# Float64 weights converted by pairs of matrices on ScalarE and VectorE, and the split of nine groups by subtraction

## The chip, the cores and the metric

The kernel runs on one core of one Trainium2 chip. The metric is the device time of one execution in microseconds (us). Engines are named as in the profile: PE is TensorE, DVE is VectorE, ACT is ScalarE, POOL is GpSimd, SP is SyncE. Each runs its own instructions in order.

## The reference

Three stages, each fed by the one before:

```python
# attention with a decaying complex state: 4 x 8 heads, 768 steps, 48 wide
S_re, S_im = (ar * S_re - ai * S_im + k[t] v[t]^T, ar * S_im + ai * S_re)
y[t] = q[t] @ S_re
# gated layer on x (3072 x 384): w_a, w_b are 384 x 1536, w_out is 1536 x 384
x2 = ((x @ w_a) * (x @ w_b)) @ w_out
# eight experts, top 1: w1 is 8 x 384 x 1024, w2 is 8 x 1024 x 384
e = argmax(x2 @ w_gate);  out = gate * (relu(x2 @ w1[e]) @ w2[e])
```

The weights of the gated layer come as float64, which no engine computes with. The kernel loads them as pairs of 32-bit words and makes float32 values on the chip.

## The kernel before, in words

The 3,072 tokens go in 12 blocks of 256, and a block in two chunks of 128 (below: chunk 0 and chunk 1 of block 0). For a block, `pre` computes the decays and scales q and k with them (products at L1289); the DMA then writes transposed copies qT and kT (`turn`, L1296 to L1300, on SP's queue, and for block 0's qT on ACT's). `attn` makes the scores (sc_p, L1349), masks them, transposes k (kn_p, L1358), multiplies with v (y_p, L1388) and carries the state (kv_p, L1408). Its result x goes through the gated layer by 12 groups f of 128 hidden columns: ab_p is x with w_a and w_b of the group, g their product, and o sums g with w_out of the group. The experts follow at the end.

The 36 matrices of 128 x 384 (a, b and o of each group) pass through two functions:

- `conv` (L877) loads the raw words (384 KB, one DMA on SP) into a room, and DVE makes the float32 matrix in three passes: `shift` (L897), `low` (L900) and `sign` (L903). Rooms are places in which later the low parts of the weights stand; the first six pairs and three double rooms for o are free at once. For an o matrix the gate's weights are folded in beside it (fold): PE transposes it (wt_p, L916), ACT copies it (L920), PE multiplies it with w_gate (wg_p, L926) and ACT puts the result in eight more columns (L929).
- `parted` (L936) splits the matrix into a rounded high part and a rest for products in the faster fp32r form: ACT writes the negative (`less`, L946), a DMA of POOL adds the float32 value to it (`rest`, L949, wL), and ACT writes the high part (`high`, L953).

Block 0 uses the unsplit matrices in plain float32 (`up32`, L979, and `down32`, L985; for the first four groups chunk by chunk). All later blocks use the split ones (L971, L1014), three products for one.

The order of all instructions up to the last expert stage comes from a planner, the class `Plan` (L343): each step is added with a length, the things it reads and writes, and a wanted time `at`; `run` takes, engine by engine, the step that can start and has the smallest `at`. The table `TIMES` shifts (and stretches) `at` for kinds of steps. It holds no times of the chip; it only sets the order. `column` (L1291) copies three columns of the decays within the tile, on DVE. The last function that matters is the end of `expert`: each tile of 128 tokens of an expert's result is scaled by ACT or DVE and scattered by POOL; the very last tile is cut in halves, ACT (L818) and DVE (L819).

## Time and profile before

| | |
|---|---|
| median of 3 runs | 896.99 us (896.51, 896.99, 898.57) |
| the profiled execution | 897.96 us, its span 896.2 us, mean granted clock 0.998 |
| busy: PE, DVE, ACT, POOL | 850.6 (95%), 562.2 (63%), 479.7 (54%), 318.3 (36%) us |
| DMA | 120.28 MB, mean 134 GB/s, first tenth of the span 231 to 273 GB/s |
| chain that ended last | PE 92%, DVE 3%, DMA 3%, SP's queue 1%, ACT 1% |

The page gives the busy time of each engine and its share of the span; the digits of its second part are tenths of busy time in 40 slices of 22.4 us. PE is at 9 in all slices but the first two and the last. The timeline gives start, duration, line, operation and the idle time ahead of it in square brackets. The table of waits adds up that idle time by what ended it. In a DMA row the last number is the time from the issue to the landing of the data.

### The profile page before, as it was taken

To read this page: it belongs to the slowest core of one execution; us is meant where nothing else is said; L and a number is where in the kernel's file an instruction comes from. 1 tells how busy PE (TensorE), PEld (TensorE's weight loads), DVE (VectorE), ACT (ScalarE), POOL (GpSimd) and SP (SyncE) were. 2 spreads that over 40 slices of the span, in tenths; PEclk is the share of its full clock that TensorE was granted. 3 is DMA by queue.
4 is the path that set the end of the run, shared out by engine and by line. 5 is a ranking of instruction groups with operands and counts; after the bars stand their busy time and mean duration, and the time that the engine had idled before them with its cause. 6 is when DMAs were issued, how large, how long until landed. Compare 5 with 4: busy or idle time off the path is not lost.

```text
span 896.2 us, 20677 instructions
## 1 busy us (share of the span) xinstructions
PE 850.6 (95%) x8186; PEld 815.9 (91%) x8186; DVE 562.2 (63%) x1285; ACT 479.7 (54%) x915; POOL 318.3 (36%) x309
## 2 busy tenths in 40 slices
PE   0399999999999999999999999999999999999997
PEld 0387899999999999999999999999999999999996
DVE  6999996775647567484939576345563655455541
ACT  6478787674746456564646473224452544444441
POOL 2341441323363636354353545221123223234111
PEclk9999999999999999999999999999999999999999
DMA  9999975242324272734354453403444454454510
GB/s 253 267 273 259 231 147 151 76 112 66 115 49 131 62 221 46 193 92 124 117 154 132 93 156 81 125 2 111 156 116 128 143 161 136 144 171 125 163 61 24
DMA packets 133017, 120.28 MB, mean 134 GB/s; under 512 B 35964, under 2 KB 127434, under 8 KB 132911
## 3 DMA queue, kind: packets, MB, share of 16 engines
q1 hardware_dynamic: 121519, 100.60, 39.7%
q0 software_dynamic: 9664, 17.47, 8.4%
q8 instruction: 66, 1.08, 0.5%
q10 hardware_dynamic: 1728, 0.79, 0.4%
q14 instruction: 40, 0.33, 0.1%
HBM read 82.48 MB, written 10.61 MB: 104 GB/s over the span
## 4 chain that ended last, share of the span: by engine, by line
PE 92%; DVE 3%; DMA 3%; SPq 1%; ACT 1%; issue 0%; POOL 0%; ACTq 0%; POOLq 0%
PE ab_p L971 31%; PE o L1014 16%; PE o L810 13%; PE h_p L778 12%; PE sc_p L1349 4%; PE y_p L1388 4%; PE ab_p L979 3%; PE o L985 2%; PE kv_p L1408 2%; PE kn_p L1358 1%; PE tn_p L755 1%; DMA q<-in_q_dram 1%; DMA qT<-A 1%; DMA raw<-in_moe_w_dram 1%; DMA raw<-in_moe_w_a_dram 1%; SPq L1138 0%
## 5 line engine op out<-in xcount | busy, mean ns | idle before, releaser
L971 PE MATMUL ab_p<-xH,wL 128*128 128x256 f32 x792 | 221.7, 280 | 0.0
L971 PEld LDWEIGHTS ab_p<-xH,wL 128*128 128x128 f32 x792 | 148.9, 188 | 0.0
L1005 POOL TENSOR_TENSOR gL<-g,gH 128x256 fp32r<-128x256 f32 x96 | 80.0, 835 | 172.3 <-ACT gH L1001 165.6
L994 ACT COPY g<-ab_p 128x256 f32<-128x256 f32 x132 | 48.9, 371 | 136.8 <-PE ab_p L971 124.0
L997 DVE TENSOR_TENSOR g<-g,ab_p 128x256 f32<-128x256 f32 (+1 forms) x148 | 60.5, 409 | 94.0 <-ACT g L994 92.0
L971 PE MATMUL ab_p<-xH,waH 128*128 128x256 f32 x396 | 114.0, 288 | 0.0
L971 PE MATMUL ab_p<-xL,waH 128*128 128x256 f32 x396 | 111.4, 281 | 0.0
L971 PE MATMUL ab_p<-xL,wbH 128*128 128x256 f32 x396 | 110.9, 280 | 0.0
L971 PE MATMUL ab_p<-xH,wbH 128*128 128x256 f32 x396 | 110.8, 280 | 0.0
L1014 PE MATMUL o<-woH,gH 128*128 128x392 f32 x264 | 96.5, 365 | 0.0
L1014 PE MATMUL o<-wL,gH 128*128 128x392 f32 x264 | 90.0, 341 | 0.0
L1014 PE MATMUL o<-woH,gL 128*128 128x392 f32 x264 | 89.9, 341 | 0.0
L810 PE MATMUL o<-w2H,h 128*128 128x384 f32 (+3 forms) x312 | 86.4, 340 | 0.0
L778 PE MATMUL h_p<-sH,w1H 128*128 128x256 f32 (+6 forms) x240 | 77.4, 322 | 0.2 <-DVE hL L789 0.2
L778 PE MATMUL h_p<-sH,w1L 128*128 128x256 f32 (+6 forms) x240 | 76.9, 321 | 0.0
L778 PE MATMUL h_p<-sL,w1H 128*128 128x256 f32 (+6 forms) x240 | 76.8, 320 | 0.0
L971 PEld LDWEIGHTS ab_p<-xH,waH 128*128 128x128 f32 x396 | 74.8, 189 | 0.9 <-issue 0.2
L1001 ACT ACTIVATE gH<-g 128x256 fp32r<-128x256 f32 x132 | 54.5, 413 | 38.5 <-DVE g L997 35.3
L971 PEld LDWEIGHTS ab_p<-xL,waH 128*128 128x128 f32 x396 | 74.7, 189 | 0.4
L971 PEld LDWEIGHTS ab_p<-xH,wbH 128*128 128x128 f32 x396 | 75.0, 189 | 0.0
L971 PEld LDWEIGHTS ab_p<-xL,wbH 128*128 128x128 f32 x396 | 74.8, 189 | 0.0
L824 POOL DMA_INDIRECT out_dram<-ye,ids x29 | 29.9, 1032 | 112.1 <-ACT ye L823 99.9
(211 smaller groups left out, 2135.8 us busy)
## 6 DMA issues: line engine op xcount, KB each, us to landing
raw<-in_moe_w_dram SPq DMA_DIRECT2D x64, 384.0 KB, 3.4
x2d<-x SPq DMA_DIRECT2D x24, 196.0 KB, 3.3
q<-in_q_dram SPq DMA_DIRECT2D x24, 192.0 KB, 4.5
v<-in_v_dram SPq DMA_DIRECT2D x24, 192.0 KB, 4.1
raw<-in_moe_w_a_dram SPq DMA_DIRECT2D x12, 384.0 KB, 6.8
raw<-in_moe_w_b_dram SPq DMA_DIRECT2D x12, 384.0 KB, 5.4
raw<-in_moe_w_out_dram SPq DMA_DIRECT2D x12, 384.0 KB, 7.4
wL<-a POOLq DMA_DIRECT2D x24, 192.0 KB, 6.8
```

Source lines behind the costliest of these rows:

```text
L778: nc.tensor.matmul(out=t, lhsT=lh[:, o:o + 128], rhs=rh[:, kk], start=n == 0, stop=n == 8)
L810: nc.tensor.matmul(out=G["o", c], lhsT=lh, rhs=rh, start=f == 0 and n == 0, stop=f == NH - 1 and n == len(ops) - 1)
L824: d = nc.gpsimd.indirect_dma_start(out, bass.IndirectOffsetOnAxis(ap=ids[0:r, c:c + 1], axis=0), y[0:r], None, bounds_check=NT - 1, oob_is ...
L971: nc.tensor.matmul(out=t[:, i], lhsT=lh[:, kk * 128:(kk + 1) * 128], rhs=rh[:, kk], start=n == 0, stop=n == 8)
L979: nc.tensor.matmul(out=t[:, i], lhsT=A32[nm, f][:, kk * 128:(kk + 1) * 128], rhs=xT["F", 0][:, kk, cs[0]:cs[0] + len(cs)].rearrange("p c t ...
L994: nc.scalar.copy(out=G["g", j, f], in_=G["ab", j, f][:, 0])
L997: nc.vector.tensor_tensor(out=G["g", j, f], in0=G["g", j, f], in1=G["ab", j, f][:, 1], op=ALU.mult)
L1001: nc.scalar.activation(out=G["H", j, f], in_=G["g", j, f], func=ACTF.Copy)
L1005: eng.tensor_tensor(out=G["L", j, f], in0=G["g", j, f], in1=G["H", j, f].bitcast(F32), op=ALU.subtract)
L1014: nc.tensor.matmul(out=G["o", j, c], lhsT=lh[:, c * C:(c + 1) * C], rhs=rh, start=f == first and n == 0, stop=f == last and n == 2)
L1349: nc.tensor.matmul(out=S["p", hg][:, h], lhsT=pq["k", j][:, hg * 4 + h, c, :], rhs=pq["q", j][:, hg * 4 + h, c, 0:C], start=True, stop=True)
L1388: nc.tensor.matmul(out=t[q4 * 32:q4 * 32 + 32, kk], lhsT=a, rhs=b, start=f0, stop=f1)
```

## The change

1. `conv` treats a and b of a group as one matrix "ab" of 768 columns (two raw loads into one room), and o alone. There are six rooms of each kind (FIRST = 3 and three reused). DVE's three passes become an ACT pass and two of DVE: ACT turns the low word into a float in a fixed binade whose last bits are the three that the high word lacks (`tail`), and DVE xors the shifted high word in (`body_`) and then sign and top bits (`head`).
2. `parted`, for the groups f < 9, drops the accumulating DMA: ACT writes the high part, DVE subtracts it (`taken`). Groups 9 to 11 keep the old way, a pair at a time.
3. `column` goes from DVE to ACT. The last output tile is scaled whole by ACT.
4. The table `TIMES` has other numbers and other entries, so that most of the order of the first 120 us is new.

```diff
+DIRECT = 9
-FIRST = (6, 3)
+FIRST = 3
+BY_TAIL = {"ab": 0, "o": 0}
+TAIL = (7.49 * 2.0 ** -55, -2.0 + 2.0 ** -23)
...
-    ('pre', 0, 1, 0): (-32.6, 1),
-    ('pre', 0, 1, 1): (18.2, 2.16),
+    ('pre', 0, 1, 0): (-175.1, 1),
+    ('pre', 0, 0, 2): (-165.1, 1),
...
-                            elif e == NE - 1 and c == nt - 1:
-                                nc.scalar.activation(out=y[0:r, 0:DM // 2], in_=G["o", c][:, 0:DM // 2], func=ACTF.Copy, scale=gt[0:r, c])
-                                nc.vector.tensor_scalar(out=y[0:r, DM // 2:DM], in0=G["o", c][:, DM // 2:DM], scalar1=gt[0:r, c], scalar2=None, op0=ALU.mult)
...
+        SIZE = dict(ab=2 * 384, o=384 + NE)
+        def room(f):
+            return f if f < FIRST else FIRST + (f - FIRST) % (NF // 2 - FIRST)
...
+            def tail():
+                held()
+                nc.scalar.activation(out=K["a"].bitcast(F32), in_=K["lo"], func=ACTF.Copy, scale=TAIL[0], bias=TAIL[1])
+            def body_():
+                nc.vector.scalar_tensor_tensor(out=K["a"], in0=K["hi"], scalar=3, in1=K["a"], op0=ALU.logical_shift_left, op1=ALU.bitwise_xor)
+            def head():
+                nc.vector.scalar_tensor_tensor(out=K["a"], in0=K["hi"], scalar=0x7FFFFFFF, in1=K["a"], op0=ALU.bitwise_or, op1=ALU.bitwise_xor)
...
+            if nm in BY_TAIL and f >= BY_TAIL[nm]:
+                P.add("ACT", on("ACT", m), tail, kind="tail", r=mine, w=[slot], at=at)
+                P.add("DVE", on("DVE", m), body_, kind="conv", r=mine, w=[slot], at=at)
+                P.add("DVE", on("DVE", m), head, kind="conv", r=mine, w=[slot, done], at=at)
...
+            def taken():
+                nc.vector.tensor_tensor(out=W["L", nm, f], in0=A32[nm, f], in1=W[nm, f][0], op=ALU.subtract)
+            if f < DIRECT:
+                P.add("ACT", on("ACT", n), high, kind="less", r=[slot, ("A32", nm, f)], w=[mine, ("W", nm, f)], at=at)
+                P.add("DVE", on("DVE", n), taken, kind="taken", r=[slot, ("A32", nm, f), ("W", nm, f)], w=[own, ("L", nm, f)], at=at + SPLIT[2])
+                return
...
-                        nc.vector.tensor_copy(out=(ld[x, j] if x == "q" else PT[x, j])[:, :, lo:hi, C:C + 1], in_=T("A")[:, :, :, C - 1:C])
+                        nc.scalar.copy(out=(ld[x, j] if x == "q" else PT[x, j])[:, :, lo:hi, C:C + 1], in_=T("A")[:, :, :, C - 1:C])
```

The order changes most in the first 50 us. On SP, before, from the last two raw loads of the first twelve (L890 and L888 are raw loads; the first six kT are the transposed copies of chunk 0, the next six those of chunk 1):

```order
L890 DMA raw<-in_moe_w_b_dram 128x3x256
L888 DMA raw<-in_moe_w_out_dram 128x768
L1300 DMA kT<-Bt 16x8x128 x3
L1300 DMA kT<-k 16x8x128 x3
L890 DMA raw<-in_moe_w_a_dram 128x3x256
L890 DMA raw<-in_moe_w_b_dram 128x3x256
L888 DMA raw<-in_moe_w_out_dram 128x768
L890 DMA raw<-in_moe_w_a_dram 128x3x256
L1300 DMA kT<-Bt 16x8x128 x3
L1300 DMA kT<-k 16x8x128 x3
L890 DMA raw<-in_moe_w_b_dram 128x3x256
L888 DMA raw<-in_moe_w_out_dram 128x768
```

In the change (raw loads are L908 and L906) the same place, up to chunk 0's kT (im is an input of the attention):

```order
L908 DMA raw<-in_moe_w_b_dram 128x3x256
L906 DMA raw<-in_moe_w_out_dram 128x768
L1195 DMA im<-in_a_im_dram 128x3x256
L908 DMA raw<-in_moe_w_a_dram 128x3x256
L908 DMA raw<-in_moe_w_b_dram 128x3x256
L906 DMA raw<-in_moe_w_out_dram 128x768
L908 DMA raw<-in_moe_w_a_dram 128x3x256
L908 DMA raw<-in_moe_w_b_dram 128x3x256
L906 DMA raw<-in_moe_w_out_dram 128x768
L1355 DMA kT<-Bt 16x8x128 x3
L1355 DMA kT<-k 16x8x128 x3
```

Four raw loads of groups 4 and 5 that stood behind chunk 0's kT, and two that stood behind chunk 1's, now stand ahead of both, so that eighteen raw loads and not twelve come first.

On PE, before, from the second fold to kn_p (a_383 is o1, wt_p and wg_p are the fold):

```order
L916 MATMUL wt_p<-ident,a_383 128x128 [waits DVE_49]
L916 MATMUL wt_p<-ident,a_383 128x128 x2
L926 MATMUL wg_p<-wg,wt 32x8 [waits Activation_49]
L926 MATMUL wg_p<-wg,wt 32x8 x11
L1349 MATMUL sc_p<-qT,kT 128x128 [waits DMAHW4_49,DMAHW3_49,DMAHW5_49,DMAHW2_49,DMAHW6_49,DMAHW1_49,DMAHW7_49,DMAHW0_49,PE_49]
L1349 MATMUL sc_p<-qT,kT 128x128 x3
L1349 MATMUL sc_p<-qT,kT 128x128 [waits PE_49]
L1349 MATMUL sc_p<-qT,kT 128x128 x3
L1358 MATMUL kn_p<-ident,kT 128x96 [waits Activation_49]
L1358 MATMUL kn_p<-ident,kT 128x96 x3
L1358 MATMUL kn_p<-ident,kT 128x96 [waits DVE_49]
L1358 MATMUL kn_p<-ident,kT 128x96 x3
```

In the change, from the third fold (a_330 is o2, a_342 is o3):

```order
L955 MATMUL wt_p<-ident,a_330 128x128 [waits DVE_49,PE_49]
L955 MATMUL wt_p<-ident,a_330 128x128 x2
L965 MATMUL wg_p<-wg,wt 32x8 [waits Activation_49]
L965 MATMUL wg_p<-wg,wt 32x8 x11
L1404 MATMUL sc_p<-qT,kT 128x128 [waits DMAHW4_49,DMAHW3_49,DMAHW5_49,DMAHW2_49,DMAHW6_49,DMAHW1_49,DMAHW7_49,DMAHW0_49,PE_49]
L1404 MATMUL sc_p<-qT,kT 128x128 x3
L955 MATMUL wt_p<-ident,a_342 128x128 [waits DVE_49,PE_49]
L955 MATMUL wt_p<-ident,a_342 128x128 x2
L1404 MATMUL sc_p<-qT,kT 128x128 [waits DVE_49]
L1404 MATMUL sc_p<-qT,kT 128x128 x3
L1413 MATMUL kn_p<-ident,kT 128x96 [waits Activation_49]
L1413 MATMUL kn_p<-ident,kT 128x96 x3
```

One more fold stands ahead of the first scores, and the transposes of a fourth stand between their two halves.

On DVE, in the change, around the scans of block 0 (L1289, whose results scale q and k; L930 and L933 are the two xors, L1001 the subtraction; a_233 and a_288 are pairs, a_307 is o1):

```order
L1279 SCALAR_TENSOR_TENSOR Bt<-X,Bt 128x3x128 [waits DVE_49]
L930 SCALAR_TENSOR_TENSOR a_288<-raw,a_288 128x768 [waits DMAHW7_49,DMAHW0_49,Activation_49]
L1001 TENSOR_TENSOR wL<-a_233,wabH_256 128x768
L1289 SCALAR_TENSOR_TENSOR X<-zeros,X 128x128 [waits Activation_49]
L1289 SCALAR_TENSOR_TENSOR X<-zeros,X 128x128 x2
L933 SCALAR_TENSOR_TENSOR a_288<-raw,a_288 128x768 [waits DVE_49]
L1328 SCALAR_TENSOR_TENSOR X<-X 128x3x128 [waits Activation_49]
L930 SCALAR_TENSOR_TENSOR a_307<-raw,a_307 128x384 [waits DMAHW1_49]
L1329 TENSOR_SCALAR carry<-X 128x3 [waits DVE_49]
L933 SCALAR_TENSOR_TENSOR a_307<-raw,a_307 128x384 [waits DVE_49]
L1289 SCALAR_TENSOR_TENSOR X<-zeros,carry,X 128x128 [waits DVE_49]
L1289 SCALAR_TENSOR_TENSOR X<-zeros,carry,X 128x128 x2
```

The xors of a pair and the first subtraction now stand ahead of the first scans; before, the 128x384 pass L897 of b0 and a reduction stood just ahead of them.

## Rows read from the trace of the kernel before

**Rows 1.** The page, part 1: busy us, share of the span, instructions.

```profile
PE 850.6 (95%) x8186; PEld 815.9 (91%) x8186; DVE 562.2 (63%) x1285; ACT 479.7 (54%) x915; POOL 318.3 (36%) x309
```

**Rows 2.** Waits of PE: waited for, us in total, times, longest.

```profile
PE wt_p L916 <- DVE a L903: 33.9, 2, 26.3
PE ab_p L979 <- ACT x L1393: 1.1, 1, 1.1
PE sc_p L1349 <- issue: 0.5, 1, 0.5
PE ab_p L979 <- DVE g L997: 0.5, 1, 0.5
```

**Rows 3.** Timeline of PE: start, us, line, operation, count [idle before].

```profile
37.35 0.90 PE L916 MATMUL wt_p<-ident,a 128*128 128x128 f32 x3 [7.65 <-DVE a L903]
38.82 0.51 PE L926 MATMUL wg_p<-wg,wt 128*32 128x8 f32 x24 [0.57 <-ACT wt L920]
39.36 3.76 PE L1349 MATMUL sc_p<-qT,kT 96*128 96x128 f32 x16
...
47.52 1.60 PE L979 MATMUL ab_p<-x,a 128*128 128x128 f32 x12 [1.08 <-ACT x L1393]
...
52.64 1.95 PE L1349 MATMUL sc_p<-qT,kT 96*128 96x128 f32 x16
```

**Rows 4.** DMA: SP's issue, landings of windows 20.9:22 and 32.8:33.3, the page's wL.

```profile
20.92 1.03 SPq L888 DMA_DIRECT2D raw<-in_moe_w_out_dram  x1
...
raw<-in_moe_w_out_dram SPq DMA_DIRECT2D x1, 384.0 KB, 9.9
...
kT<-k SPq DMA_DIRECT2D x1, 64.0 KB, 2.0
...
wL<-a POOLq DMA_DIRECT2D x24, 192.0 KB, 6.8
```

**Rows 5.** Windows: busy us of PE, PEld, DVE, ACT, POOL; clock, DMA share, GB/s.

```profile
25.00:30.00 5.00, 1.38 (x27) 0.92 (x27) 4.11 (x9) 1.77 (x5) 3.34 (x3) 1.00 1.08 350
30.00:35.00 5.00, 0.00 (x0) 0.00 (x0) 5.00 (x13) 3.06 (x5) 1.28 (x1) 1.00 0.69 155
60.00:80.00 20.00, 19.50 (x172) 14.81 (x171) 19.72 (x46) 16.71 (x38) 5.89 (x6) 1.00 1.04 280
```

**Rows 6.** Timeline of DVE, conversion of two matrices.

```profile
32.59 0.62 DVE L897 TENSOR_SCALAR a<-raw 128x384 uint32<-128x384 uint32 x2
33.13 1.02 DVE L900 SCALAR_TENSOR_TENSOR a<-raw,a 128x384 uint32<-128x384 uint32 x2
34.06 1.35 DVE L1289 TENSOR_TENSOR A<-q,X 128x384 f32<-128x384 f32 x1
```

**Rows 7.** Groups, busy and mean ns: DVE subtraction and ACT roundings.

```profile
L678 DVE TENSOR_TENSOR w1L<-raw,w1H 128x768 fp32r<-128x768 f32 x32 | 30.7, 958 | 6.8 <-ACT w1H L677 6.1
...
L677 ACT ACTIVATE w1H<-raw 128x768 fp32r<-128x768 f32 x32 | 26.9, 840 | 2.1 <-DMA raw<-in_moe_w_dram 2.1
...
L946 ACT ACTIVATE wL<-a 128x384 fp32r<-128x384 f32 (+1 forms) x36 | 18.2, 526 | 1.1 <-DVE k L1289 0.8 <-DVE a L903 0.3
```

**Rows 8.** Timeline of PE, places of one wg_p and one wt_p.

```profile
67.70 0.38 PE L926 MATMUL wg_p<-wg,wt 128*32 128x8 f32 x24
68.00 1.58 PE L985 MATMUL o<-a,g 128*128 128x392 f32 x4
69.43 0.49 PE L916 MATMUL wt_p<-ident,a 128*128 128x128 f32 x3
69.75 1.50 PE L979 MATMUL ab_p<-x,a 128*128 128x128 f32 x12
```

**Rows 9.** Timeline of all engines behind the last matmuls.

```profile
889.62 0.42 ACT L818 ACTIVATE ye<-o,gt 120x192 f32<-120x192 f32 x1 [7.79 <-PE o L810]
890.08 0.42 DVE L819 TENSOR_SCALAR ye<-o,gt 120x192 f32<-120x192 f32 x1 [4.01 <-ACT ye L818]
890.81 1.05 POOL L824 DMA_INDIRECT out_dram<-ye,ids  x1 [3.48 <-DVE ye L819]
```

More of the change, by code (lines that the diff above doesn't have):

```diff
@@ L874, in fast, with behind @@
-        late = [("ab", f) for f in range(FIRST[0], NF)] + [("o", f) for f in range(FIRST[1], NF // 2)]
-        rooms += [late[i % len(late)] for i in range(3 * NF - len(rooms))]
-        def conv(i, f, src, nm, at):
+        SIZE = dict(ab=2 * 384, o=384 + NE)
+        def behind(nm, k, dt, n):
+            return wts.tile([128, 2 * SIZE[nm]], dt, tag=f"l{nm}{k}", name=n)
+        for nm in SIZE:
+            for f in range(NF):
+                wts.tile([128, SIZE[nm]], F32R, tag=f"h{nm}{f}", name=f"w{nm}H{f}")
+            for h in range(NF // 2):
+                behind(nm, h, F32R, "wL")
@@ L885, in load @@
[L885 to L892 removed]
+            slot, mine = ("s",) + (to or (nm, NF)), [("sl", nm, 2 * room(f)), ("sl", nm, 2 * room(f) + 1)]
@@ L1304, in mul @@
                     for x in "Aq":
-                        add("DVE", column(x), ks("A", x), [("column", x, lo)], weight=0.16)
+                        add("ACT", column(x), ks("A", x), [("column", x, lo)], weight=0.2)
                 add(e, times, ks(src, "Cc" if c2 == 0 else "F"), ks(t))
```

223 lines of the change are left out of this document (124 added, 99 removed).

## The prediction

> **What bounds the kernel now.** I read the page's busy times first: TensorE is busy for 850.6 of 896.2 us [rows 1]. Only PE's clock of work matters, then, and nothing is won on another engine unless PE waits for it. The waits of PE come next [rows 2]: 33.9 us for the last pass of a weight's conversion (L903, all of it before 39.4 us), and after that 1.1, 0.5 and 0.5 us in three single places. The whole rest of the 800 us runs without a wait worth a row. So a change that keeps PE's instructions can move the time in three places only: the instant at which PE starts for good, the few waits after it, and the end behind the last matmul. Both programs give PE the same matmuls, 6,546 by the two orders and of the same shapes (8,186 records in the profile, where an fp32 one counts twice), in another order. Hence the sum below has just these three places, with no term for work.
>
> The instant is read in PE's timeline [rows 3]: the fold of o1 (three transposes wt_p at 37.35, twelve wg_p at 38.82), then the scores of the first chunk, sc_p, from 39.36, and no gap over 0.1 us until a 1.08 us wait at 47.52. The 7.65 us of idle time ahead of wt_p name DVE: the start is set by o1's conversion. The scores' other inputs are the transposed copies kT and qT, made by DMA. The last kT of the first chunk was issued from 32.8 on and landed 2.0 us after its issue [rows 4]: at about 35. They were ready over 4 us before PE used them. Twelve raw weights of 384 KB stood ahead of them on SP; the last of these was issued at 20.92 and landed 9.9 us later, at 30.8 [rows 4]. The DMA engines were full before that (share 1.08, 350 GB/s, from 25 to 30), and not in the next 5 us (0.69) [rows 5]. From 60 to 80 DVE is busy 19.72 us of 20 and ACT 16.71 [rows 5].
>
> **The change part by part.** *Loads.* The rooms of the raws are now six pairs and six single ones, and SP issues eighteen raws, a to o of groups 0 to 5, ahead of the first kT. Six more raws of 393,216 bytes take 1.12 us each at the 350 GB/s of 25 to 30, 1.40 at the 280 of 60 to 80 [rows 5]: 6.7 to 8.4 us. One accumulating DMA of 192 KB that fell into that stretch is gone [rows 4]; it reads its target too, so I count it between half a raw and a whole one, about 1 us. The last raw then lands at 30.8 + 6.7 - 1.0 = 36.5, at most 38.2. Behind it come the chunk's twelve transposes of 64 KB: 0.19 to 0.25 us each by the same rates, 2.3 to 3.0 us. The scores' inputs are complete at 38.8 to 41.2. The slack of 4 us is used up and the two paths to the start are now about equal.
>
> *Conversion ahead of the start.* PE folds three output groups, o0 to o2, before the scores, not two. Up to the last xor of o2, DVE makes three pairs and three single matrices and takes one subtraction (wL from a, L1001). Before it made six matrices there. Per matrix that was L897 at 0.27 us (two from 32.59 to 33.13) and two passes at 0.465 (two from 33.13 to 34.06) [rows 6], 1.2 us, so 7.2 in all. A pass over 768 columns has its nearest row in L678, 0.958 us [rows 7]; less the 0.085 by which consecutive ones overlap (0.55 against 0.465) that is 0.87. Now: six passes of 768, six of 384 and one subtraction, 6 x 0.87 + 6 x 0.465 + 0.87 = 8.9 us. DVE had little idle time there (5.00 us busy of 5 from 30 to 35, 4.11 before [rows 5]), so o2's fold ends 1.7 us later than o1's did: PE starts at 41.1. Four short copies (`column`) leave DVE in that stretch; I set what they give against the new waits of the xors for ACT, which must make the low bits first. The start therefore lies between 39.4 (copies count, raws land at the fast rate) and 42.5 (slow rate, and the last transposes wait for a place on their queue). I take 41.1, where the DVE path ends and which lies within the DMA path's ends: **+1.7 us**, from 0 to +3.1.
>
> *The third fold* is done while PE would be idle: later PE has one wt_p (0.32 us from 69.43 to the next row) and one wg_p (0.30 from 67.70) less [rows 8]: **-0.6**.
>
> *Half speed.* The sixteen passes of the first sc_p took 3.76 us, those of the second chunk 1.95 [rows 3]. The first stretch after the start thus runs at the lower of the clock's two levels. The new order has the same kind of unbroken work there, so it pays the same; a wait among the first scores might lengthen it, which is in the upper end.
>
> *Known waits.* At 47.52 PE waited 1.08 us for the copied x; the new order puts the first kv_p and a wt_p between y_p and this ab_p, and some 0.8 us of the wait is filled. The 0.5 of ab_p behind the product g [rows 2] loses its place. Together **-1.3**. The 0.5 of issue I leave.
>
> *New waits.* The order has five new places where PE takes a result just made: the second half of sc_p, behind o3's wt_p; a wg_p between the kn_p; ab_p of groups 2 and 3 behind their xors; the first product with the split weights, which now needs a subtraction behind ACT's rounding. The nearest rows are the recorded waits of this sort, 0.5 to 1.1 us [rows 2]; at five places 0 to 4 us. I take **+2.0**, 0.4 each, near the smaller of these rows, because PE runs behind its inputs for most of that time.
>
> *Later conversion.* Over all groups DVE loses 36 x 1.2 = 43.2 us, gets 24 x 0.87 + 24 x 0.465 = 32.0 and the nine groups' subtractions, 9 x 0.87 + 9 x 0.48 = 12.2: +1.0, which the 24 short copies outweigh. Hidden behind PE as long as DVE is no later than now; where that cover goes, see the second rival. ACT loses 72 roundings of 0.526 us [rows 7], 0.44 if they overlap as DVE's do (31.7), and gets tails and roundings in 768 columns at 0.84 - 0.085 = 0.755 [rows 7] and in 384 at 0.44: 14.3 for the twelve pairs of tails, 14.3 for the rounding, 3.6 for the three groups that keep the old way, and the copies at about 0.1 each, in sum +2.9 us. With 16.71 of 20 busy [rows 5] ACT has room for it: 0. The Trainium skill speaks against this move: its page "ScalarE: Activation LUTs", section "Rules for kernel authors", gives multiply and add to VectorE and not to ScalarE, because VectorE is faster per element. The rows bear out the speed, 0.84 us for 768 columns against 0.62 for two L897 of 384 [rows 6, 7]; but what counts is who has room. If ACT were the one that PE waits for, the sum would be 2.9 us higher. The thirty accumulating DMAs that go free POOL and the DMA queues, neither of which PE waits for: 0.
>
> *Tail.* The last output tile was scaled in two halves, one after the other: ACT at 889.62, DVE only at 890.08, the scatter issued at 890.81 [rows 9]. Each half took 0.42. Whole, it takes ACT about 0.55 (192 columns take 0.42, 768 take 0.84 [rows 7, 9]); with the 0.31 from the last half's end to the scatter that is 0.86 in place of 1.19: **-0.3**.
>
> **Sum:** 1.7 - 0.6 - 1.3 + 2.0 - 0.3 = +1.5 us. The profiled execution took 897.96 (its span 896.2 and 1.8 around it) and would take 899.5. It is 0.97 above the median of the runs shown, so against that: 896.99 + 1.5 = **898.5 us**. A measurement of this kernel tells about 0.2%, 1.8 us, from no change. The forecast is no change that can be told, with a lean to slower; its own range is 897 to 900.5.
>
> **Rivals.** *The start does not move* (faster). In rows 5 the DMA engines have room from 30 to 35, and the raws are issued earlier now because nothing blocks SP; if the copies' time on DVE counts in full and the xors don't wait for ACT, the start stays at 39.4 to 39.7. With inputs that early all three recorded waits go (1.1 + 0.5 + 0.5) and hardly any comes: 0.3 - 0.6 - 2.1 + 0.3 - 0.3 = -2.4, or -3.0 without the first and the fourth term: 894.0 to 894.6. Against it: the kT stand behind the raws on the same queue, and the subtraction stands ahead of the scans that make k.
>
> *DVE or ACT becomes the engine that PE waits for up to some 115 us* (slower). Every weight now crosses ACT, DVE, ACT and DVE, in order, where it crossed DVE and then ACT beside POOL's DMA. DVE has 0.28 us of room in 20 [rows 5], about 1 us in the 70 up to the last subtraction. Once its idle time for ACT's tails exceeds that, PE gets the excess: 0.2 to 0.4 us in each of twelve groups is 2.4 to 4.8 us, less the 1 us of room, so 900 to 902.3, and with the start at its late end 903. For it: DVE's full row. Against: ACT's tails need only the raw, which is early. An ACT pass over uint32 words with a gap between them is shown by no row; at twice the time it would add 14 us to ACT and give the same picture at its upper end.
>
> *The new waits don't come* (the change's first order is as quiet as the old one): 1.7 - 0.6 - 1.3 - 0.3 = -0.5, with some tenths of waits 896.5 to 897.
>
> **How the numbers follow.** The forecast has 0.50 (0.30 of it within 0.2% of 896.99, that is below 898.8, 0.20 above). The start that doesn't move has 0.19, of which 0.17 is below 895.2 (it may end between). DVE or ACT as the bound has 0.21, all slower. No new waits has 0.10, of which 0.02 is below. So faster 0.19, same 0.40, slower 0.41. The range reaches from the middle of the first rival to the upper part of the second, 894.3 to 902.6, and leaves out about 0.1 on each side.
>
> **What would show it.** In PE's timeline: sc_p's first row at 40.5 to 42 (39.4 to 39.9 for the first rival); twelve transposes landing after the eighteenth raw; three folds ahead of sc_p. In PE's waits after it: several rows of 0.2 to 0.9, together near 2.5 us; over 5, with DVE or ACT named between 60 and 115, the second rival holds. At the end: one ACT row of about 0.55 and the scatter 0.3 us sooner after the last matmul. I would be wrong in kind if PE's busy time or its spacing in the long middle differed.

## The result: 7.4 us slower, and the profile after

The changed kernel takes 904.44 us (median of 5 runs, 902.87 to 907.5), the kernel before, beside it, 896.99 (5 runs, 896.51 to 898.75). The ratio is 1.0075 with a 95% interval of 1.0058 to 1.0092: slower, by more than the forecast's whole range (894.3 to 902.6) allowed. The profiled execution is the longest of the five, 907.5 us with a span of 905.4. It is 9.5 us above the profiled execution before.

The page's part 1, to be laid beside [rows 1]:

```profile
PE 852.5 (94%) x8186; PEld 815.0 (90%) x8186; DVE 563.5 (62%) x1216; ACT 486.9 (54%) x923; POOL 292.7 (32%) x279
```

PE has the same 8,186 records and 1.9 us more busy time; the others moved the way that the edit asks for (POOL 25.6 us less, ACT 7.2 and DVE 1.3 more). So the time is in PE's waits and in the pace of its work, not in its amount. The table of waits of PE (waited for, us in total, times, longest) beside [rows 2]:

```profile
PE wt_p L955 <- DVE a L933: 33.4, 3, 22.3
PE wg_p L965 <- ACT wt L959: 3.7, 3, 1.6
PE o L1069 <- POOL gL L1060: 2.4, 3, 2.0
PE ab_p L1023 <- DVE g L1052: 2.2, 1, 2.2
PE h_p L804 <- DVE hL L815: 2.0, 1, 2.0
PE sc_p L1404 <- issue: 0.8, 1, 0.8
PE rk_p L663 <- DVE oh L640: 0.6, 1, 0.6
PE ab_p L1023 <- DVE xL L1457: 0.4, 1, 0.4
```

The first two rows lie ahead of the first scores. Behind them stood 2.1 us of waits before; now there are 6.4 in the rows of o, ab_p, sc_p, rk_p, and 2.0 more for h_p in the expert stage. None of the three large ones (2.0 of the 2.4 for gL, 2.2, 2.0) was in the forecast. PE's timeline at the head (start, us, line, operation, count, idle time before) beside [rows 3]:

```profile
38.39 0.88 PE L955 MATMUL wt_p<-ident,a 128*128 128x128 f32 x3 [7.00 <-DVE a L933]
40.82 0.51 PE L965 MATMUL wg_p<-wg,wt 128*32 128x8 f32 x24 [1.56 <-ACT wt L959]
41.53 2.05 PE L1404 MATMUL sc_p<-qT,kT 96*128 96x128 f32 x8 [0.20 <-DMA qT<-A]
43.37 0.85 PE L955 MATMUL wt_p<-ident,a 128*128 128x128 f32 x3
44.37 2.08 PE L1404 MATMUL sc_p<-qT,kT 96*128 96x128 f32 x8
...
47.32 0.51 PE L965 MATMUL wg_p<-wg,wt 128*32 128x8 f32 x24 [0.24 <-DVE sm L1408]
...
50.30 1.50 PE L1463 MATMUL kv_p<-v,kn 128*32 128x48 f32 x48
```

The start moved from 39.36 to 41.53, 2.2 us. Beside [rows 3] it falls into three parts: the last fold's wt_p came at 38.39 in place of 37.35 (1.0 us), its wg_p waited 1.56 us for ACT's copy in place of 0.57 (1.0), and sc_p waited 0.20 for qT. The copy stood on ACT behind the issues of qT:

```profile
40.29 0.48 ACT L959 COPY wt<-wt_p 128x384 f32<-128x384 f32 x1 [4.50 <-DMA qT<-q]
```

The second thing to see is the pace. The 48 passes of kv_p take 1.50 us here at 50.30; in the kernel before the same 48 took 0.88:

```profile
49.05 0.88 PE L1408 MATMUL kv_p<-v,kn 128*32 128x48 f32 x48
```

In the change PE still runs at the lower of its two levels (1.2 and not 2.4 GHz): the trace's first record of the full granted clock is at 52.5, 11.0 us after the first scores, where before it was at 45.5, 6.1 us after them. In that stretch lie o3's wt_p between the two halves of sc_p and a wait of 0.24 us. (The windows read 1.00 ahead of that record too; there the passes' own times have to be read.)

The lower level comes back once. Windows of before and then after: start, end, length, busy us of PE, PEld, DVE, ACT, POOL, granted clock, DMA share, GB/s:

```profile
135.00:140.00 5.00, 5.00 (x40) 5.00 (x39) 2.61 (x5) 4.72 (x11) 0.00 (x0) 1.00 0.66 178
```

```profile
135.00:140.00 5.00, 2.77 (x15) 2.57 (x14) 1.56 (x3) 3.84 (x6) 1.72 (x1) 0.79 0.85 267
140.00:145.00 5.00, 5.00 (x40) 4.91 (x38) 4.04 (x7) 3.84 (x6) 0.00 (x0) 0.87 0.47 133
```

Behind the 2.23 us wait of ab_p at 137.77 the passes come 0.21 us apart until 141.26. What held ab_p stands in ACT's timeline:

```profile
136.16 0.84 ACT L1264 ACTIVATE A<-re 128x768 f32<-128x768 f32 x1 [3.24 <-DMA qT<-q]
136.91 0.35 ACT L1049 COPY g<-ab_p 128x256 f32<-128x256 f32 x1
```

The first decay step of block 3 (A<-re) stands ahead of the gate's copy and waits 3.24 us for a transposed copy of block 2. The gate's copy, which PE needs, has nothing to wait for there but its place. The same picture on POOL at 481, for the wait at 483.25:

```profile
472.62 0.98 POOL L686 DMA_INDIRECT idtab<-tok,posu  x1 [0.94 <-DVE acc L675]
...
481.14 0.98 POOL L686 DMA_INDIRECT idtab<-tok,posu  x1 [4.37 <-DMA idtab<-tok,posu]
482.15 1.05 POOL L1060 TENSOR_TENSOR gL<-g,gH 128x256 fp32r<-128x256 f32 x1
```

The second index scatter waits 4.37 us until the first, issued at 472.62, has landed; the low part gL, which the next product needs, stands behind it.

Where the 9.5 us went by time: the first product of the expert stage (h_p), behind which the order is the old one, starts at 653.66, before at 646.14. So 7.5 us are lost up to there, and 2.0 in one wait behind a late expert weight. That last one is not all the change's: the same kernel again had 0.70 there, the kernel before 0.2. For the 7.5, two windows from the first score to h_p, before and then after (columns as above):

```profile
39.36:646.14 606.78, 604.52 (x6653) 578.07 (x6653) 406.27 (x901) 352.91 (x662) 239.62 (x218) 1.00 0.50 130
```

```profile
41.53:653.66 612.13, 605.03 (x6626) 576.04 (x6626) 404.70 (x843) 355.93 (x659) 214.27 (x192) 1.00 0.43 118
```

PE is idle for 7.1 us of its window in place of 2.3, and busy for 605.0 in place of 604.5. So the start gives 2.2, the waits 4.8 and the work 0.5, in sum 7.5. The 0.5 hides larger parts, which I work out from the starts of the passes in the two traces, waits left out. The passes at the lower level took 6.8 us longer than as many of the same kinds at the full level, before 3.2: 3.6 more. The third fold, done ahead of the scores, saves 0.7 behind them. At the full level ab_p and o together took 478.2 us in place of 481.7, 3.5 less, and the other products 1.1 more. Why ab_p and o ran closer together is shown by no run.

The tail did what was forecast: ACT's whole tile takes 0.58 us, and the scatter is issued 0.31 behind its end.

```profile
899.00 0.58 ACT L846 ACTIVATE ye<-o,gt 120x384 f32<-120x384 f32 x1 [7.79 <-PE o L836]
899.89 1.05 POOL L847 DMA_INDIRECT out_dram<-ye,ids  x1 [3.19 <-ACT ye L846]
```

From the start of the last matmul to the end it is 6.73 us, before 7.00.

### The profile page after: what moved, and what is told of

The parts are those of the page before. It is cut to its first block, busy times and chain, and to the rows that moved or that the text cites. A ratio compares the mean times of both kernels' runs of the same rounds, so it can differ in the third digit from the quotient of the medians.

```text
span 905.4 us, 20607 instructions
## 1 busy us (share of the span) xinstructions
PE 852.5 (94%) x8186; PEld 815.0 (90%) x8186; DVE 563.5 (62%) x1216; ACT 486.9 (54%) x923; POOL 292.7 (32%) x279
## 4 chain that ended last, share of the span: by engine, by line
PE 77%; issue 8%; DMA 4%; DVE 4%; POOL 3%; SPq 2%; ACT 1%; POOLq 0%; ACTq 0%; DVEq 0%
PE ab_p L1023 28%; PE o L1069 14%; PE o L836 9%; PE h_p L804 8%; PE sc_p L1404 5%; PE y_p L1443 4%; PE ab_p L1031 3%; DMA raw<-in_moe_w_b_dram 2%; PE kv_p L1463 2%; PE kn_p L1413 1%; PE o L1037 1%; PE tn_p L781 1%; POOL out_dram L847 1%; DMA qT<-A 1%; POOL gL L1060 1%
## 5 line engine op out<-in xcount | busy, mean ns | idle before, releaser
L1023 PE MATMUL ab_p<-xH,wabH 128*128 128x256 f32 x792 | 226.3, 286 | 2.2 <-DVE g L1052 2.2
L1023 PE MATMUL ab_p<-xL,wabH 128*128 128x256 f32 x792 | 221.8, 280 | 0.4 <-DVE xL L1457 0.4
L1023 PEld LDWEIGHTS ab_p<-xH,wabH 128*128 128x128 f32 x792 | 150.2, 190 | 5.2 <-DVE g L1052 3.1
L1023 PEld LDWEIGHTS ab_p<-xL,wabH 128*128 128x128 f32 x792 | 149.8, 189 | 0.8 <-DVE xL L1457 0.6
L1052 DVE TENSOR_TENSOR g<-g,ab_p 128x256 f32<-128x256 f32 x132 | 54.9, 417 | 120.2 <-ACT g L1049 119.8
L1069 PE MATMUL o<-woH,gH 128*128 128x392 f32 x264 | 93.4, 354 | 0.0
L813 ACT ACTIVATE h<-h_p 128x384 fp32r<-128x384 f32 (+4 forms) x48 | 24.5, 510 | 76.4 <-PE h_p L804 76.4
L815 DVE SCALAR_TENSOR_TENSOR h<-h_p,h 128x384 fp32r<-128x384 f32 (+1 forms) x48 | 26.7, 556 | 62.4 <-ACT h L813 62.3
L836 PE MATMUL o<-w2L,h 128*128 128x384 f32 (+3 forms) x168 | 56.8, 338 | 0.0
L836 PEld LDWEIGHTS o<-w2H,h 128*128 128x128 f32 (+3 forms) x312 | 56.3, 186 | 0.5
```

The lines of the kernel that those rows point to most:

```text
L836: nc.tensor.matmul(out=G["o", c], lhsT=lh, rhs=rh, start=f == 0 and n == 0, stop=f == NH - 1 and n == len(ops) - 1)
L1023: nc.tensor.matmul(out=t[:, i], lhsT=lh[:, kk * 128:(kk + 1) * 128], rhs=rh[:, kk], start=n == 0, stop=n == 8)
L1052: nc.vector.tensor_tensor(out=G["g", j, f], in0=G["g", j, f], in1=G["ab", j, f][:, 1], op=ALU.mult)
L1069: nc.tensor.matmul(out=G["o", j, c], lhsT=lh[:, c * C:(c + 1) * C], rhs=rh, start=f == first and n == 0, stop=f == last and n == 2)
```

## The experiments

The runs were made in six groups, each on one chip with the kernel before beside it; all ratios are to that. In most of them a few lines behind the planner take one step out of the finished order and put it behind another step; nothing else is changed. MOVE holds pairs of step numbers (which, behind which):

```python
for a, b in MOVE:
    i = [n for _, n, _ in out].index(a)
    x = out.pop(i)
    out.insert([n for _, n, _ in out].index(b) + 1, x)
```

### Do the waits belong to the order?

**after_again**: no edit.

> The changed kernel once more, for its spread and a second profile. The theory: of the 10.5 us of waits and half-speed work behind the start, the wait at 137.8 us (2.2 us, with 1.7 us of slower passes behind it) belongs to the order and comes again, within 0.5 us; the waits at 245, 431, 483 and 678 us (0.6, 0.8, 2.0, 2.0) hang on single slow transfers and move or vanish. Then the sum of waits behind the start is 5 to 11 us, other than in the first profile in the second half of the span. The rival, that all of them belong to the order: the same waits in the same places. Time 903 to 907.5 by both.

Measured 905.58 us, 1.0074 [1.0054, 1.0094]. The waits came back at the same places and sizes: 0.23 at 47.4, 2.31 at 138.7, 0.58 at 246.2, 1.10 at 432.4, 2.08 at 484.5. Only the 2.0 for an expert weight shrank, to 0.70. So the late waits are the order's own, and my expectation that they are single late transfers was wrong for all but that one.

**late_new3**: the kernel before, whose table gets the change's entries for blocks 3 and later, and nothing else.

```diff
-    ('v', 3): (-41, 1),
-    ('attn', 3, 'PE'): (33.2, 0.77),
...
+    ('pre', 3, 0, 0): (183.3, 1),
+    ('attn', 3, 'PE'): (-83.3, 4.0826),
...
```

> The kernel before, with the new planned times for blocks 3 and later alone; conversion, loads and the first 160 us as before. If the new order of the later blocks is what lets slow transfers reach PE, waits of PE appear behind 160 us, 1 to 4 us in sum, and the time is 898 to 901. If the later blocks' order costs nothing and all of the loss comes from conversion and the first 160 us, the time is that of the kernel before within 1 us (896.5 to 898).

Measured 901.73 us, 1.0037 [1.0018, 1.0055]: 3.3 us lost with the old conversion and the old head. New or longer waits of PE stand at 144.9 (0.85, before 0.55 at 144.6), 186.2 (0.63) and 428.25:

```profile
428.25 1.02 PE L1356 MATMUL sc_p<-qT,kT 96*128 96x128 f32 x7 [1.84 <-DMA qT<-q]
```

So the new entries of the later blocks cost time without the new conversion. But this is a mixed table, new entries behind old ones (best_old4 below is another, and loses more), and its waits are other ones than in the change: how much of the change's loss these entries make is not shown by it.

### The wait at 138

**swap_sqre**: ACT's A<-re of block 3 goes behind the gate's copy, MOVE = ((682, 595),).

> One instruction of ACT moved: the square of block 3's decay (A<-re), which waits for a transfer, now stands behind the next gate copy of block 1 and not ahead of it. The theory, that this one wait holds PE at 137.8 us: the wait shrinks from 2.2 to under 0.5 us, the clock stays at its higher level there, and the time falls by 2.5 to 4 us against the changed kernel of this job. The rival, that DVE's and ACT's load in the conversion stretch sets PE's pace there: the wait comes back at the next gate copy, and the time falls by under 1 us.

Measured 904.57 us, 1.0076 [1.0054, 1.0097]: nothing gained. The wait went on to the next result in line:

```profile
141.22 0.90 PE L1423 MATMUL kn_p<-ident,kT 96*128 96x96 f32 x4 [1.96 <-DVE sm L1418]
```

The cause is one step further. DVE's subtraction of a group waits for ACT's rounding, which is still behind A<-re, and the masks stand behind it and behind two scalings of block 3:

```profile
137.74 0.96 DVE L1011 TENSOR_TENSOR wL<-a,wabH 128x768 fp32r<-128x768 f32 x1 [3.76 <-ACT wabH L1005]
...
140.48 0.68 DVE L1418 TENSOR_TENSOR sm<-sc_p,causal 128x512 f32<-128x512 f32 x1
```

**pre3_late** moves the whole group: ACT's A<-re and the two steps with it behind the rounding, DVE's scalings of block 3 behind both masks.

```diff
+MOVE = (
+    (685, 491),
+    (684, 491),
+    (682, 491),
+    (845, 651),
+    (693, 651),
+    (689, 651),
+    (844, 651),
+    (688, 651),
+)
```

> The changed kernel with block 3's first decay steps behind what block 1 and 2 need: on ACT A<-re stands behind the gate copy and the next rounding, on DVE the two passes of block 3's X stand behind both masks of block 2. The theory, that the order puts an instruction that waits for a late transfer ahead of PE's inputs on both engines: the wait at 138 to 141 us (2.0 to 2.3 in three profiles) falls below 1 us, the clock stays high there, and the time falls by 2 to 4 us. The rival, that DVE and ACT are short of time there (they lost some 9 us of DVE in idle time from 40 to 62): a wait of the same size comes a few us later and the time falls by under 1 us.

Measured 902.82 us, 1.0030 [1.0013, 1.0046]. The wait at 138 is gone (0.15 and 0.45 us are left at 143.7 and 155.3) and with it the fall of the clock.

### The half speed at the head, and the scatter

**fold3_back**: o3's fold goes out of the middle of the first scores, behind y_p: MOVE = ((198, 391), (197, 391), (196, 128), (195, 128)).

> The changed kernel with o3's fold (wt_p, its copy, wg_p) moved from between the first scores to behind the first y_p; nothing else is moved. The theory: the 0.24 us wait of that wg_p at 47.3 us broke PE's unbroken work and kept TensorE at the lower of its two levels until 52.5 to 53.6, where it reached the higher one 6.2 us after the start in the kernel before. Without the wait the full clock comes at 47 to 48.5 and the passes up to 53 take about 2 us less; new waits at kv_p may take up to 1.2 of that. The time falls by 1 to 2.5 us. The rival, that the longer half-speed stretch follows from the later start alone: the clock still comes at 52 or later, and the time stays within 0.5.

Measured 903.38 us, 1.0031 [1.0015, 1.0046]. PE's timeline:

```profile
41.48 3.75 PE L1417 MATMUL sc_p<-qT,kT 96*128 96x128 f32 x16 [0.17 <-DMA qT<-A]
45.02 0.97 PE L1426 MATMUL kn_p<-ident,kT 96*128 96x96 f32 x8
```

The sixteen passes of sc_p run without a break, and kn_p behind them takes 0.97 us for eight. The kernel before took 1.49:

```profile
42.90 1.49 PE L1358 MATMUL kn_p<-ident,kT 96*128 96x96 f32 x8
```

The full level comes at 45.3, 3.8 us after the first scores. This is one execution, and the instant varies: in the three profiles of combo below, which has the same move, it comes 8.7, 6.1 and 3.9 us after them; in the seven profiles of the change's conversion that leave the fold in its place (the change three times, swap_sqre, pre3_late, idtab_late, raws_behind) 8.9 to 12.0. So the fold's place shortens the stretch on the whole, by no fixed amount. Part of the gain goes into a new wait of kv_p for ACT's copy kn at 48.91 (0.96).

**idtab_late**: the second index scatter of each pair goes behind the next three instructions of POOL.

```diff
+        for a in [o["n"] for o in ops if o["kind"] == ("scatter", 1)]:
+            i = [n for _, n, _ in out].index(a)
+            j = [q for q in range(i + 1, len(out)) if ops[out[q][1]]["e"] == "POOL"][2]
+            out.insert(j, out.pop(i))
```

> The changed kernel with the second of each block's two scatters of ids (POOL) moved behind the next three POOL instructions. The theory: the second scatter waits for the first one's landing, 8 us at 474 us, and PE's low part gL stands behind it on POOL; moved, the wait of 1.5 to 2.1 us at 482 to 484 us goes, and the small ones at 334 and 402 us with it, and the time falls by 1.5 to 2.5 us. The rival, that POOL is only late there with everything else: another wait takes its place and the time stays within 0.7 us.

Measured 904.06 us, 1.0035 [1.0019, 1.0052]. The waits for gL at 334 and 483 are gone, 0.25 at 401 stays, and the wait for g at 137 (1.83 us, with the lower level until 140.7) is not.

These three were on one chip without the changed kernel beside them, so what each gave is not to be read from their ratios. That is done with all three together.

### The three moves together

**after_third**: no edit, the yardstick.

> The changed kernel as it is, as the yardstick for the three runs beside it on the same chip. Theory (the order's own waits): 6 to 8.5 us over the kernel before, with the same waits in the same places (0.24 us of wg_p at 47 us, 2.2 near 138, 0.6 near 246, 1 near 432, 2 near 484). Rival (the waits are chance on two chips): places or sizes differ by over half.

Measured 905.80 us, 1.0059 [1.0035, 1.0084]; waits at the same places, 1.91 us at 136.8 this time without a fall of the clock behind it.

**combo**: MOVE holds the pairs of fold3_back and pre3_late, and the scatters move as in idtab_late.

> Three moves together: the third output group's late fold goes behind y_p, the decay step and the scalings of block 3 go behind the gate work, each second index scatter goes three steps of POOL later. Theory (the loss sits in single waits and in the half speed that follows them, and they add): 5 to 7 us below the changed kernel on the same chip, so 1 to 3 above the kernel before, of which 2 are the later start; no half speed after 46 us. Rival (a wait removed comes back at the next result that PE takes): within 2 us of the changed kernel, with new waits of 3 us or more in sum.

Measured 901.97 us, 1.0008 [0.9987, 1.0029], 3.8 us below after_third and 1.2 above the kernel before beside it. Repeated on that chip it took 900.65, 1.0015 [0.9998, 1.0032] (combo_again), and 900.05, 1.0011 [0.9995, 1.0026] (combo_third).

> The three moves together once more, as the yardstick for the two runs beside it. From the first such run: 0 to 2.5 us over the kernel before on the same chip, full clock from 51 us on, no drop after it.

> The three moves alone a third time, as the yardstick for the run beside it: 0 to 2.5 us over the kernel before, the first sc_p at 41.5 us.

Combo's table of waits, the first two rows behind those of the folds:

```profile
PE tn_p L807 <- issue: 1.0, 1, 1.0
PE sc_p L1430 <- issue: 0.9, 1, 0.9
```

The longest wait is 1.02 us there and 1.12 in combo_again. Moving 24 steps (the twelve pairs of MOVE and twelve scatters) takes back 3.8 of the 5.0 us by which the change was slower on that chip. Most of the loss thus sat in places of the order. In this pair of profiles it was the waits: the full level came at 50.5 in combo and at 50.7 in after_third, and PE's idle time from the first score to h_p fell from 7.2 to 4.0 us. How the 3.8 us divide among the three moves is not shown.

**best_old4**: the moves of fold3_back and pre3_late, and for blocks 4 and later the table entries of the kernel before.

> The first two moves (third fold, block 3), and the table's entries for blocks 4 and later are those of the kernel before. Theory (the later blocks' new entries cost 3 us by themselves): no wait of o for gL near 334 and 484, those of 246 and 432 gone or halved, and the time 0.5 to 2.5 us below the three moves alone. Rival (a mixed table is a third order with waits of its own): new waits of 1 us or more behind 200 us in other places, the time 0 to 3 us above the three moves alone.

Measured 908.06 us, 1.0093 [1.0068, 1.0118], beside combo_again 7.4 us slower. The rival held: a mixed table is a third order, with waits of its own between 239 and 275 us (1.82 for gL, 1.84 and 2.00 for g) and the lower level from 250.0 to 256.9. It also leaves the scatters where they were, which combo moves, so the 7.4 us are not the table's alone.

### The two parts of the edit, each undone in the same order

**conv_dve**: DVE converts alone, in the three old passes, at the places of the two xors.

```diff
             def tail():
-                held()
-                nc.scalar.activation(out=K["a"].bitcast(F32), in_=K["lo"], ...)
+                pass
             def body_():
-                nc.vector.scalar_tensor_tensor(out=K["a"], in0=K["hi"], scalar=3, ...)
+                shift()
+                low()
             def head():
-                nc.vector.scalar_tensor_tensor(out=K["a"], in0=K["hi"], scalar=0x7FFFFFFF, ...)
+                sign()
```

> Same order, but the float64 words are converted by DVE alone in its three old passes at the place of the two xors; ACT's pass is left out. Theory (the two-engine conversion does what it is made for, DVE is the fuller engine): DVE gets some 9 us more up to 90 us (12 x 0.5 and 12 x 0.27), PE's first sc_p comes at 43 to 44.5 us, new waits of PE name DVE between 48 and 90, and the time is 3 to 8 us above the changed kernel. Rival (the wait of DVE for ACT's pass costs what the pass saves): sc_p within 0.7 us of 41.5 and the time within 1.5 us of the changed kernel, or below it.

Measured 913.66 us, 1.0139 [1.0105, 1.0173], 7.9 us above after_third, as the theory had it. The first scores came at 42.78, a little sooner than expected, and the waits stand for the most part later than it had them:

```profile
PE ab_p L1031 <- DVE g L1045: 2.0, 3, 1.4
PE ab_p L1023 <- DVE g L1052: 1.8, 1, 1.8
...
PE ab_p L1023 <- DVE xL L1457: 1.3, 1, 1.3
```

They name DVE, in six places between 73 and 145 us. So in this order ScalarE's pass does what it is for. The rule of the Trainium skill that the forecast weighed (page "ScalarE: Activation LUTs", section "Rules for kernel authors": add and multiply belong on VectorE, with a figure for bf16 and one source), taken by itself, speaks for this run, and it was the slower one. But the order was made for the new passes: the old passes in their own order, the kernel before, took 900.77 us on that chip, less than either. What the two conversions are worth in an order made for each is not shown.

**sub_dma**: the first nine groups get their low parts in the old way (ACT writes the negative, here directly behind the high part, and a DMA of POOL adds the value).

```diff
             def high():
...
-                    place()
+                    less()
...
             def taken():
-                nc.vector.tensor_tensor(out=W["L", nm, f], in0=A32[nm, f], in1=W[nm, f][0], op=ALU.subtract)
+                rest()
```

> Same order, but the low parts of the first nine groups are made in the old way: ACT writes the negative and the high part, a DMA of POOL adds the value; DVE's eighteen subtractions are left out. Theory (PE does not wait for DVE's whole load but for single results in the order): DVE 12 us less, ACT 12 us more, time within 2 us of the changed kernel, waits at 138, 246, 432 and 484 unchanged. Rival (DVE, full from 60 to 80 us, is the bound): 3 us or more below the changed kernel, with DVE's idle time between 60 and 115 up by 10 us.

Measured 925.42 us, 1.0272 [1.0238, 1.0306], 19.6 above after_third. Neither side had that. ACT's roundings now wait for the accumulating DMAs to land, and the copies that PE needs stand behind them:

```profile
106.25 0.84 ACT L995 ACTIVATE wabH<-a 128x768 fp32r<-128x768 f32 x1 [2.90 <-DMA wL<-a]
```

```profile
109.91 0.86 PE L1463 MATMUL kv_p<-v,kn 128*32 128x48 f32 x24 [2.41 <-ACT kn L1418]
```

PE waits 6.3 us for kn in four places and falls to the lower level three times. An order made for a subtraction has no room for a DMA in its place. What the subtraction would be worth in an order made for the DMA is not shown by it.

### The start

**raws_behind**: the raw loads o4, a5, b5 and o5 go behind chunk 0's kT on SP, MOVE = ((217, 72), (213, 72), (212, 72), (204, 72)).

> On SP four of the eighteen raw loads (o4, a5, b5, o5) now stand behind chunk 0's kT; nothing else is moved. If the transposes behind the raws set the start, as the prediction had it with DVE beside them, the fold's copy on ACT is no longer behind waiting transposes and sc_p starts 0.8 to 1.5 us sooner (40.0 to 40.7 in place of 41.5), and the time falls by as much. If o2's conversion on DVE alone sets it, sc_p stays within 0.4 us of 41.5 and the time within 0.5.

Measured 905.79 us, 1.0096 [1.0069, 1.0123]. The first scores came at 42.01, waiting for qT:

```profile
42.01 1.20 PE L1417 MATMUL sc_p<-qT,kT 96*128 96x128 f32 x4 [1.28 <-DMA qT<-A]
```

The last of chunk 0's six qT was issued on ACT at 36.59, behind two of the four moved raws (35.66 and 36.30), so these were ahead of it again. Beside after_again (905.58 us, scores at 41.62) nothing was gained, and the run does not tell the two sides apart.

**early**: combo, and a4 and b4 behind chunk 0's kT, o4 to o5 behind chunk 1's, group 4's conversion behind the masks, o2's fold behind the first scores.

> The three moves, and the start undone: the raw loads of a4, b4 go behind chunk 0's kT and o4, a5, b5, o5 behind chunk 1's (with the ACT pass of group 4 and its two xors behind the masks' work), and o2's fold goes behind the first scores. Theory (the start is late because six more raws lie ahead of the transposes and o2's fold ahead of the scores): the first sc_p comes at 38.5 to 39.8 us, 1.7 to 3 sooner; at most 1.5 us of that is given back at the ab_p of groups 3 and 4, so 1 to 2.5 us below the three moves alone, about the time of the kernel before. Rival (the scores are late for their own inputs, the products on DVE and POOL behind the conversion): sc_p at 41 or later with a DMA or DVE named, and the time within 0.7 us of the three moves alone.

Measured 900.95 us, 1.0015 [0.9997, 1.0033], beside combo_again the same. The rival's signs came, a DMA named and the scores at 41 or later:

```profile
41.16 3.76 PE L1443 MATMUL sc_p<-qT,kT 96*128 96x128 f32 x16 [9.68 <-DMA qT<-A]
```

ACT issues the first qT at 31.80; in the kernel before it was 26.63. Chunk 0's product on DVE that it is made of (A<-q) starts at 31.24 here, before at 26.04: the attention's own steps stand behind the conversion. That is only a part of it, for the loads were not out of the way. The last of chunk 0's six qT was issued at 36.11, behind the raws a4 and b4, which SP issues at 35.38 and 36.01. It took 5.0 us to land, at 41.07, where the fourth, issued at 34.38, took 2.6:

```profile
qT<-q ACTq DMA_DIRECT2D x1, 64.5 KB, 5.0
```

```profile
31.00:36.00 5.00, 0.48 (x24) 0.39 (x24) 4.86 (x10) 3.41 (x6) 1.15 (x2) 1.00 0.48 118
36.00:41.00 5.00, 0.00 (x0) 0.00 (x0) 5.00 (x9) 0.00 (x0) 0.00 (x0) 1.00 0.99 265
```

The DMA share doubles when the two raws and chunk 1's first copies are under way (0.48, then 0.99). At 2.6 us the last qT would have landed at 38.7, by my estimate. So the late steps and the raws share the wait; the run does not separate them.

**early2**: DVE's scan and products of chunk 0 go ahead of the conversion of groups 1 to 3.

> The run before last of the start (raw loads and o2's fold moved back) left PE waiting for the last qT, whose issue began at 31.8 us, 5 us later than in the kernel before. Here chunk 0's scan and products on DVE go ahead of the conversion of groups 1 to 3 and of the first subtraction, the ACT passes and o1's fold behind the issues of qT. Theory (the start is set by the attention's own products, which stand behind the conversion): qT issues from 27 to 29 us, the first sc_p at 38 to 40 us, 1.2 to 3 sooner, and the time 1 to 2.5 us below the version without this move (1.0015 of the kernel before), so 1 us under to 0.5 us over the kernel before. Rival (the conversion pushed back is then late for the products behind the scores): the first sc_p is early, but waits of 1 to 3 us in sum come at the folds and at ab_p between 42 and 60 us, and the time stays within 0.7 us.

Measured 902.74 us, 1.0039 [1.0020, 1.0059]. A miss of mine: on ACT the first issue of qT was left behind a step of chunk 1 and came at 31.29 again; the scores came at 40.90, behind o1's fold.

**early3**: as early2, and on ACT all six issues of qT directly behind chunk 0's products, o1's fold and chunk 1's steps behind them.

> In the run before, the first qT was still issued at 31.3 us, though its product was done at 28.8: on ACT it stood behind a step of chunk 1 that waits for DVE, and the scores then waited for o1's fold on ACT. Here all six issues of qT stand directly behind chunk 0's products, o1's fold behind them, chunk 1's scan and its ACT steps after that. Theory (the start is set by chunk 0's products and what ACT does ahead of qT's issue): qT issued from 28.5 to 33 us, the first sc_p at 36 to 38.5 us, 3 to 5 sooner than in the change; of that 1 to 4 us come back as waits between 40 and 62 us, since DVE has the same conversion to do by then (it is the fuller engine there), so the time is 0 to 2.5 us below the three moves alone. Rival (the start costs nothing as such, because PE is caught by DVE's conversion a few us later anyway): sc_p is early, PE's position at 62 us is within 0.7 us of that of the three moves alone, and so is the time.

Measured 901.42 us, 1.0019 [1.0004, 1.0034], beside combo_third 1.4 us slower. PE's timeline:

```profile
35.54 3.75 PE L1467 MATMUL sc_p<-qT,kT 96*128 96x128 f32 x16 [1.78 <-DMA kT<-k]
39.08 0.85 PE L1476 MATMUL kn_p<-ident,kT 96*128 96x96 f32 x4
44.79 0.90 PE L1476 MATMUL kn_p<-ident,kT 96*128 96x96 f32 x4 [4.87 <-DVE sm L1471]
```

```profile
38.70 1.42 DVE L993 SCALAR_TENSOR_TENSOR a<-raw,a 128x768 uint32<-128x768 uint32 x2
40.04 1.42 DVE L996 SCALAR_TENSOR_TENSOR a<-raw,a 128x768 uint32<-128x768 uint32 x2
...
44.05 1.28 DVE L1471 TENSOR_TENSOR sm<-sc_p,causal 128x512 f32<-128x512 f32 x2
```

The scores start 6.2 us sooner than in combo_third, and all of it is given back: the masks stand behind eight passes of conversion on DVE, PE waits 4.87 us, and runs longer at the lower level. At the first o of block 0 it is 1.5 us behind (59.60 against 58.09). So in this order, with DVE's conversion between the scores and what follows, the earlier start was worth nothing. An order that also puts the masks ahead of these passes was not tried, so what a start is worth there is open. No version ran below the kernel before; combo is the nearest, 0.8 to 1.5 thousandths above it in three measurements, each within its interval.

## Why the prediction was wrong

**The step that failed is the term "new waits", +2.0.** It counted five new places at the head, 0.4 us each, and took the rest from the profile before: "The whole rest of the 800 us runs without a wait worth a row." That was true of the old order only. The change replaces the table that made it, with entries for every block. Measured: PE is idle for 7.1 us between the first score and h_p, where the sum comes to 3.0 (the old 2.3, less 1.3, and this term). At the five head places stand 0.24 us for the wg_p and, at the first split products, 0.44 for the low part of x, not of a weight; nothing over 0.2 at the others. Outside them stand 2.2 at 138, 2.0 at 483, 0.8 at 431, 0.6 at 246. combo shows that moving the steps at the head, at 138 and at the scatters gives back 3.8 us, and late_new3 that entries for the later blocks can cost 3.3 without the new conversion.

**Half speed, put at nothing, failed too: "it pays the same" was wrong.** The start of the scores is the same kind of work, but o3's fold and the wait of 0.24 us cut it. The lower level lasted 11.0 us in place of 6.1, and came back for 3.4 us behind the wait at 138; from the starts of the passes that cost 3.6 us more than before. With the fold moved back the first stretch lasted 3.8 to 8.7 us in four profiles (fold3_back and combo three times), without the move 8.9 to 12.0 in seven. The forecast had this only as an upper end.

**The start was right in size, not in reason.** 41.53 measured, 41.1 forecast. The sum put all of +1.7 down to o2's conversion on DVE. That path gives 1.0 us (wt_p at 38.39); another 1.0 is the fold's copy on ACT behind the issues of qT, which the forecast did not have, and 0.2 the wait for qT. The path of the loads was about as long as forecast: the eighteenth raw landed at 36.8 (36.5 forecast), and the scores waited for qT last. (A transposed copy of 64 KB takes 0.23 us at the forecast's lower rate, not 0.25, which changes its upper end by 0.2.) early shows a step that the forecast left out, the attention's products behind the conversion. So +1.7 came near 2.2 in part by luck. Whether an earlier start would have been worth its size is not shown: in early3's order it came back as waits.

**Known waits, -1.3:** both are gone, as said, 1.6 us in all. The 0.5 of issue, at 144.6 before, is gone as well, and another of 0.8 stands at 431. The 2.23 at 138 is a wait of the same kind as the old one for g, at a new place.

**Third fold, -0.6, and tail, -0.3:** the fold comes out as -0.7 from the starts of its passes, the tail as -0.27.

**No term for work:** right in the amount. But ab_p and o ran 3.5 us shorter than before, for which the sum has nothing; without that the loss would have been larger.

**Later conversion, 0:** right where it was claimed, though ACT's busy time grew by 7.2 us over the whole kernel and not by 2.9. From 60 to 100 us DVE is busy 39.65 of 40 us and ACT 33.87, and no wait of PE between 60 and 115 names either for over 0.3 us. The second rival, DVE or ACT as the bound of that stretch, did not happen, and its time (900 to 903) was nearest only by chance. At the head it has a part: DVE is busy 10.81 of 20 us from 40 to 60 (before 17.27), 3.0 of the idle time in two waits for ACT's pass, so the room that the change makes on DVE comes where the order does not use it.

```profile
48.53 0.56 DVE L930 SCALAR_TENSOR_TENSOR a<-raw,a 128x384 uint32<-128x384 uint32 x1 [1.36 <-ACT a L927]
...
54.00 0.96 DVE L930 SCALAR_TENSOR_TENSOR a<-raw,a 128x768 uint32<-128x768 uint32 x1 [1.59 <-ACT a L927]
```

**Still open:** how the 3.8 us of combo divide among its three moves, why ab_p and o ran closer together, and whether the 1 to 1.5 us that combo stays above the kernel before are anything: they lie within the intervals.

## What to carry to other kernels

A table or planner that sets the order is part of the change, over the whole kernel: the quiet stretches of a profile belong to the old order, and each place where a waiting instruction stands ahead of a short one that the bounding engine needs has to be looked for anew, in every block. Read the queue of the engine that is waited for, not the wait: at 138 and at 483 the instruction that PE's input hung on stood directly behind one that waited for a DMA to land. And an earlier start is worth only what the next engine in line can follow, as early3 shows.

## What the runs showed of the hardware

- The same kernel reached the full level at different distances from its first scores: 8.7, 6.1 and 3.9 us in three profiles of combo, 11.0, 12.0 and 8.9 in three of the change. So the price of the stretch ahead of it is not read from one profile.
- Behind waits of about 2 us the lower level came back in some executions (near 138: 2.23, 2.31 and 1.83 us; 1.96 in swap_sqre; 1.82 at 249 in best_old4) and not in others (1.91 in after_third and 1.94 in fold3_back near 136; 2.01, 2.08 and 1.97 at 483 in the three profiles of the change). So the price of such a wait is not read from its length alone.
- ScalarE takes 914 ns for 768 columns of 32-bit words read with a gap of one word, against 842 for 768 columns of float32 (L995). The forecast feared twice the time.

```profile
L927 ACT ACTIVATE a<-raw 128x768 f32<-128x768 uint32 x12 | 11.0, 914 | 1.8 <-DMA raw<-in_moe_w_b_dram 1.7
...
L995 ACT ACTIVATE wabH<-a 128x768 fp32r<-128x768 f32 x12 | 10.1, 842 | 0.0
```

- The index scatters and the loads of their table took 1.9 to 8.2 us from issue to landing (median 3.1). Where one scatter waits for the one before, everything behind it on POOL is put off by that.
